# A cached-attention decode kernel on one core: each K and V tile loaded by two transfers, one from SP and one from ScalarE

## The chip, the core and the metric

The kernel runs on one core of a Trainium2 chip. The metric is the device time of one execution in microseconds (us); less is better. Engines are named as in the profile: PE (TensorE matmul), PEld (its weight load), DVE (VectorE), ACT (ScalarE), POOL (GpSimd) and SP (SyncE). SPq and ACTq are the instructions by which SP and ScalarE start DMA transfers.

## The reference

One token goes through a pre-norm attention layer with a cache and a gated feed-forward layer, all in float32. The attention, cut to what matters:

```python
B, Sq, D = 1, 1, 640
H, Sk, Dh = 32, 8192, 192
q = (layernorm(x) @ wq).reshape(B, Sq, H, Dh)           # one query row for each head
scores = einsum("bhqd,bhkd->bhqk", q, k_cache) * Dh ** -0.5
p = softmax(scores)
o = einsum("bhqk,bhkd->bhqd", p, v_cache)
h = x + o.reshape(B, Sq, H * Dh) @ wo
out = h + ((relu(hn @ W_gate) * (hn @ W_up)) @ W_down)   # hn = layernorm(h), F = 1536
```

For each of 32 heads the kernel reads 6 MB of K and 6 MB of V, and uses each element once.

## The kernel before

**Tiles.** The 8192 keys of a head are spread over 128 partitions, 64 keys of 192 numbers in each, so a K tile or a V tile is 128 x 12288 float32: 6144 KB, 48 KB in each partition. `TW` is half of a row's numbers (6144). All tiles come from one pool, `kv`, of three buffers (`kv_t`), which also holds the three pieces of wq at the start and the feed-forward weights (`ffn_a`, `ffn_b`) at the end. The output weights wo are loaded in nine pieces (`wo_t`, for groups of four heads, the last two groups of two heads) into a pool of two buffers.

**Loading.** `load_kv` (L77) takes a buffer and issues one transfer for each entry of `parts`, all from SP. Every K tile and all V tiles but the last are one transfer of 6144 KB; the last V tile is five. `load_wo` (L86) issues one transfer of 1920 KB (960 KB for the last two groups). SP does nothing but issue transfers, in order; it waits before each until the buffer is free.

**One head.** For head h+1 `head_step` (L176) multiplies the K tile by the query in four quarters of 16 keys per partition (L183, DVE), adds the two halves of each product on POOL (L184), and sums what is left on DVE (L188). Between the quarters it runs the steps of the softmax of head h (`softmax_steps`: maximum L193, its transpose on PE L195, L198, its broadcast L200, then on ScalarE the bias L202 and the exponential L205, the sum on PE L207 and its reciprocal L210). Then `values_of` (L217 on) does 32 matmuls of 128x2 by 128x384 with the V tile (L225) and ScalarE scales the result (L228). `finish_steps` brings the head's row into columns (L240, L244) and, once for each group, multiplies by wo (L254).

**What sets the order.** Instructions of one engine run in the order in which a scheduler put them; the calls `keep(...)` hold the marked DVE and PE instructions in the order of the program. The scheduler also decides which of the three buffers a tile gets, and so for what a transfer waits. In the kernel before, a V tile follows a K tile in its buffer (its transfer waits for DVE's sums, L188), and a K tile follows a V tile (its transfer waits for PE's L225).

**End.** The feed-forward weights come into two of the buffers (L294 to L298), the row is normalised and multiplied, and the result goes out (L348).

Of the kernel before, what the change touches and what calls it, by code (L numbers as in the profile page):

```python
# [14 lines left out]
def kernel(  # L15
# [12 lines left out]
    nc = tc.nc  # L28
# [9 lines left out]
    TW = R * DH  # L38
# [11 lines left out]
    kf, vf = kc[0], vc[0]  # L50
# [20 lines left out]
    for j in range(0, DJ, 2):  # L71
        n = min(2, DJ - j)
# [4 lines left out]
    def load_kv(src, h, parts):  # L77
        t = kv.tile([P, 2 * TW], F32, name="kv_t")
        v = src[h].rearrange("(p r) d -> p (r d)", p=P)
        b = 0  # L80
        for n in parts:
            nc.sync.dma_start(t[:, b:b + n], v[:, b:b + n])  # L82
            b += n
        return t

    def load_wo(gi):  # L86
        hs = GROUPS[gi]
        j = len(hs) * DH // P
        t = wts.tile([P, j, D], F32, tag="wo_t", name="wo_t")
        r0 = hs[0] * DH  # L90
        nc.sync.dma_start(t, wo[r0:r0 + len(hs) * DH, :].rearrange("(p j) n -> p j n", p=P))
        return t
# [73 lines left out]
    def query(h):  # L166
        g, i = divmod(h, HPQ)
        q = ps_q.tile([P, QB], F32, tag="q", name="q")
        nc.tensor.matmul(q[:, 0:DH], sel[:, g, :], q4[:, i * DH:(i + 1) * DH], start=True, stop=True)  # L169
        return q[:, 0:DH]  # L170
# [5 lines left out]
    def head_step(q, kt, *works):  # L176


        sc = small.tile([P, NS], F32, name="sc")
        k3 = kt.rearrange("p (r d) -> p r d", d=DH)  # L180
        parts = [(i0, k3[:, i0:i0 + SUB, :]) for i0 in range(0, NS, SUB)]
        for i0, ks in parts:
            keep(nc.vector.tensor_mul(ks, ks, q[:, None, :].to_broadcast([P, SUB, DH])))  # L183
            nc.gpsimd.tensor_add(ks[:, :, 0:HD], ks[:, :, 0:HD], ks[:, :, HD:DH])  # L184
            for w in works:
                next(w, None)
        for i0, ks in parts:
            keep(nc.vector.reduce_sum(sc[:, i0:i0 + SUB], ks[:, :, 0:HD], axis=AX.X))  # L188
        return sc

    def softmax_steps(sc, res):
        mp = small.tile([P, 1], F32, name="mp")
        keep(nc.vector.reduce_max(mp, sc, axis=AX.X))  # L193
        pt = ps_s.tile([P, 512], F32, name="ps_small")
        keep(nc.tensor.transpose(pt[0:1, 0:P], mp, ident))  # L195
        yield
        m1 = small.tile([1, 1], F32, name="m1")
        keep(nc.vector.reduce_max(m1, pt[0:1, 0:P], axis=AX.X))  # L198
        pb = ps_s.tile([P, 512], F32, name="ps_small")
        nc.tensor.matmul(pb[:, 0:1], ones[0:1, :], m1, start=True, stop=True)  # L200
        nb = small.tile([P, 1], F32, name="nb")
        nc.scalar.mul(nb, pb[:, 0:1], -SCALE)  # L202
        p = small.tile([P, NS], F32, name="p")
        rs = small.tile([P, 1], F32, name="rs")
        nc.scalar.activation(p, sc, AF.Exp, bias=nb, scale=SCALE, accum_out=rs)  # L205
        pl = ps_s.tile([P, 512], F32, name="ps_small")
        nc.tensor.matmul(pl[:, 0:1], ones, rs, start=True, stop=True)  # L207
        yield
        rl = small.tile([P, 1], F32, name="rl")
        keep(nc.vector.reciprocal(rl, pl[:, 0:1]))  # L210
        res += [p, rl]
        yield
# [8 lines left out]
    def values_of(h, p, rl, vt):  # L221
        po = pos[h % 2]
        for i in range(NP):
            g = i % NQ
            nc.tensor.matmul(po[g * Q:g * Q + 2, :], p[:, 2 * i:2 * i + 2],  # L225
                             vt[:, 2 * i * DH:(2 * i + 2) * DH], start=(i < NQ), stop=(i >= NP - NQ))
        ob = small.tile([P, 2 * DH], F32, name="ob")
        nc.scalar.activation(ob, po, AF.Copy, scale=rl)  # L228
        return ob

    def finish_steps(h, ob, oT, wo_t):

        gi, i = group_of[h]
        U = NQ // len(GROUPS[gi])
        W = DH // U
        pt = ps_s.tile([P, 512], F32, name="ps_small")
        for u in range(U):
            q0 = (i * U + u) * Q
            for k in range(2):
                nc.tensor.matmul(pt[q0:q0 + Q, 0:W], par[:, k, :], ob[:, k * DH + u * W:k * DH + (u + 1) * W],  # L240
                                 start=(k == 0), stop=(k == 1))
        yield
        s = slice(i * U * Q, (i + 1) * U * Q)
        keep(nc.vector.transpose(oT[s], pt[s, 0:W].rearrange("p (c j) -> p j c", c=Q)))  # L244
        yield
        split = h >= H - 2
        if not split and i < len(GROUPS[gi]) - 1:
            return
        if not split:
            s = slice(0, P)  # L250
        J = wo_t.shape[1]
        for j in range(J):
            for g in range(NQ):
                nc.tensor.matmul(acc[g * Q:(g + 1) * Q, :], oT[s, j, :], wo_t[s, j, g * DG:(g + 1) * DG],  # L254
                                 start=False, stop=(h == H - 1 and j == J - 1))
        yield

    sc = head_step(query(0), load_kv(kf, 0, [2 * TW]))
    done = iter(())
    for h in range(H):  # L260
        gi, i = group_of[h]
        if i == 0:
            wo_t = load_wo(gi)
            oT = small.tile([P, len(GROUPS[gi]) * DH // P, Q], F32, tag="oT", name="oT")
        sm = []
        soft = softmax_steps(sc, sm)
        if h + 1 < H:
            kt = load_kv(kf, h + 1, [2 * TW])
            vt = load_kv(vf, h, [2 * TW])
            sc = head_step(query(h + 1), kt, soft, done)  # L270
        else:
            vt = load_kv(vf, h, [TW] + [TW // 4] * 4)
        for w in (soft, done):
            for _ in w:
                pass
        done = finish_steps(h, values_of(h, *sm, vt), oT, wo_t)
# [99 lines left out]
```

## Time and profile before

| | |
|---|---|
| median of 3 runs | 1045.99 us (1045.82 to 1046.0) |
| the profiled execution's own time | 1045.67 us |
| its span in the profile | 1043.9 us |
| busy: DVE / POOL / PE / ACT | 666.0 / 440.1 / 409.2 / 45.5 us |
| bytes moved by DMA | 446.39 MB, mean 428 GB/s |
| mean granted clock of TensorE | 0.641 |

The span is what the profiler saw between the first and the last instruction; 1.8 us of the profiled execution lie outside of it. A busy share is an average over the whole span. A timeline row gives start, length, engine, line, operation, tile, and in brackets how long the engine had been idle before it and what ended that. In a table of stretches the last three columns are the granted clock, the busy share of the 16 DMA engines, and GB/s; bytes are booked to the moments in which rows start, so short stretches jump about the mean, with shares above 1 too.

### The profile page before, as it was taken

To read this page: it belongs to the slowest core of one execution; us is meant where nothing else is said; L and a number is where in the kernel's file an instruction comes from. 1 tells how busy PE (TensorE), PEld (TensorE's weight loads), DVE (VectorE), ACT (ScalarE), POOL (GpSimd) and SP (SyncE) were. 2 spreads that over 40 slices of the span, in tenths; PEclk is the share of its full clock that TensorE was granted. 3 is DMA by queue.
4 is the path that set the end of the run, shared out by engine and by line. 5 is a ranking of instruction groups with operands and counts; after the bars stand their busy time and mean duration, and the time that the engine had idled before them with its cause. 6 is when DMAs were issued, how large, how long until landed. Compare 5 with 4: busy or idle time off the path is not lost.

```text
span 1043.9 us, 7403 instructions
## 1 busy us (share of the span) xinstructions
PE 409.2 (39%) x3136; PEld 151.0 (14%) x3136; DVE 666.0 (64%) x418; ACT 45.5 (4%) x140; POOL 440.1 (42%) x139
## 2 busy tenths in 40 slices
PE   1603443343345333343432443343233444432475
PEld 0101111111112111121111111121111211111122
DVE  1086777566667766467775666677664667766551
ACT  0000000000000000000000000000000000000010
POOL 0055555344455544245553444455542455544330
PEclk9856665666666566666666666665566666656678
DMA  9999999999999999999999999999999999999997
GB/s 392 445 433 428 424 444 426 435 426 443 426 432 428 439 430 422 438 432 433 428 437 430 435 428 436 429 434 428 433 424 443 430 433 434 428 432 428 435 419 302
DMA packets 13003, 446.39 MB, mean 428 GB/s; under 512 B 1573, under 2 KB 1577, under 8 KB 3114
## 3 DMA queue, kind: packets, MB, share of 16 engines
q1 hardware_dynamic: 12824, 445.92, 99.2%
q8 instruction: 24, 0.39, 0.2%
q14 instruction: 9, 0.07, 0.0%
q10 hardware_dynamic: 146, 0.01, 0.0%
HBM read 445.91 MB, written 0.00 MB: 427 GB/s over the span
## 4 chain that ended last, share of the span: by engine, by line
DMA 62%; DVE 24%; PE 10%; issue 3%; SPq 0%; ACTq 0%; ACT 0%; DVEq 0%
DMA kv_t<-in_A_k_cache_dram 57%; DVE kv_t L183 19%; PE po L225 8%; DVE sc L188 3%; DMA xrow<-in_A_x_dram 2%; DMA ffn_b<-in_B_W_down_dram 2%; DMA ffn_a<-in_B_W_up_dram 2%; PE q L169 1%; PE qp L160 1%; DVE oT L244 1%; DVE m L198 0%; DVE rl L210 0%; DVE mp L193 0%; SPq L82 0%; PE acc L150 0%
## 5 line engine op out<-in xcount | busy, mean ns | idle before, releaser
L184 POOL TENSOR_TENSOR kv_t<-kv_t 128x1536 f32<-128x1536 f32 x128 | 438.2, 3445 | 559.6 <-DVE mp L193 247.4
L183 DVE TENSOR_TENSOR kv_t<-kv_t,q 128x3072 f32<-128x3072 f32 x128 | 427.4, 3342 | 321.1 <-DMA kv_t<-in_A_k_cache_dram 311.5
L225 PE MATMUL po<-kv_t,p 128*2 128x384 f32 x2048 | 224.4, 601 | 9.7 <-DMA kv_t<-in_A_v_cache_dram 9.7
L188 DVE TENSOR_REDUCE sc<-kv_t 128x16 f32<-128x1536 f32 x128 | 215.0, 1739 | 0.0
L195 PE MATMUL ps_small<-ident,mp 128*1 128x128 f32 x32 | 11.8, 368 | 367.6 <-DVE mp L193 367.6
L169 PE MATMUL q<-q,sel 128*128 128x192 f32 x64 | 29.6, 565 | 148.9 <-DVE kv_t L183 148.9
L225 PEld LDWEIGHTS po<-kv_t,p 128*2 128x2 f32 x2048 | 54.7, 97 | 168.9 <-issue 154.3
L195 PEld LDWEIGHTS ps_small<-ident,mp 128*1 128x1 f32 x32 | 2.5, 79 | 389.6 <-issue 355.5
L240 PE MATMUL ps_small<-ob,par 128*32 128x192 f32 (+1 forms) x144 | 44.5, 479 | 0.7 <-ACT ob L228 0.7
L200 PE MATMUL ps_small<-m,ones 1*128 1x1 f32 x64 | 18.4, 354 | 51.9 <-DVE m L198 51.9
L169 PEld LDWEIGHTS q<-q,sel 128*128 128x128 f32 x64 | 14.9, 289 | 156.1 <-DVE kv_t L183 107.5
L228 ACT ACTIVATE ob<-po,rl 128x384 f32<-128x384 f32 x32 | 18.6, 580 | 432.3 <-PE po L225 432.3
L254 PE MATMUL acc<-wo_t,oT 128*32 128x160 f32 (+1 forms) x408 | 33.5, 452 | 0.4 <-DVE oT L244 0.4
L202 ACT ACTIVATE nb<-ps_small 128x1 f32<-128x1 f32 x32 | 5.5, 171 | 495.6 <-PE ps_small L200 495.6
L200 PEld LDWEIGHTS ps_small<-m,ones 1*128 1x128 f32 x64 | 15.7, 303 | 71.8 <-DVE m L198 71.8
L207 PE MATMUL ps_small<-rs,ones 128*128 128x1 f32 x64 | 18.6, 359 | 18.9 <-ACT p L205 18.9
L254 PEld LDWEIGHTS acc<-wo_t,oT 128*32 128x32 f32 (+1 forms) x408 | 18.7, 157 | 6.9 <-DVE oT L244 1.3
L160 PE MATMUL qp<-kv_t,xn 128*32 128x512 f32 x120 | 17.4, 736 | 5.3 <-DMA kv_t<-in_A_wq_dram 4.3
L207 PEld LDWEIGHTS ps_small<-rs,ones 128*128 128x128 f32 x64 | 15.8, 308 | 24.9 <-ACT p L205 24.9
L240 PEld LDWEIGHTS ps_small<-ob,par 128*32 128x32 f32 x144 | 16.7, 153 | 16.9 <-issue 7.5
L244 DVE STREAM_TRANSPOSE oT<-ps_small 32x192 f32<-32x192 f32 (+1 forms) x32 | 11.7, 364 | 10.4 <-PE ps_small L240 9.8
L205 ACT ACTIVATE p<-sc,nb 128x64 f32<-128x64 f32 x32 | 11.1, 348 | 1.0
(72 smaller groups left out, 73.4 us busy)
## 6 DMA issues: line engine op xcount, KB each, us to landing
kv_t<-in_A_k_cache_dram SPq DMA_DIRECT2D x32, 6144.0 KB, 37.0
kv_t<-in_A_v_cache_dram SPq DMA_DIRECT2D x31, 6144.0 KB, 23.1
wo_t<-in_A_wo_dram SPq DMA_DIRECT2D x7, 1920.0 KB, 27.0
kv_t<-in_A_wq_dram SPq DMA_DIRECT2D x2, 6144.0 KB, 17.8
ffn_a<-in_B_W_up_dram SPq DMA_DIRECT2D x1, 3840.0 KB
kv_t<-in_A_wq_dram SPq DMA_DIRECT2D x1, 3072.0 KB, 39.6
kv_t<-in_A_v_cache_dram SPq DMA_DIRECT2D x1, 3072.0 KB, 31.0
kv_t<-in_A_v_cache_dram SPq DMA_DIRECT2D x4, 768.0 KB, 34.6
```

Source lines behind the costliest of these rows:

```text
L160: nc.tensor.matmul(qps[b][g * Q:(g + 1) * Q, :], xn[:, j:j + 1].to_broadcast([P, Q]), wq_ts[j][:, c0:c0 + QB], start=(j == 0), stop=(j == ...
L169: nc.tensor.matmul(q[:, 0:DH], sel[:, g, :], q4[:, i * DH:(i + 1) * DH], start=True, stop=True)
L183: keep(nc.vector.tensor_mul(ks, ks, q[:, None, :].to_broadcast([P, SUB, DH])))
L184: nc.gpsimd.tensor_add(ks[:, :, 0:HD], ks[:, :, 0:HD], ks[:, :, HD:DH])
L188: keep(nc.vector.reduce_sum(sc[:, i0:i0 + SUB], ks[:, :, 0:HD], axis=AX.X))
L200: nc.tensor.matmul(pb[:, 0:1], ones[0:1, :], m1, start=True, stop=True)
L207: nc.tensor.matmul(pl[:, 0:1], ones, rs, start=True, stop=True)
L225: nc.tensor.matmul(po[g * Q:g * Q + 2, :], p[:, 2 * i:2 * i + 2], vt[:, 2 * i * DH:(2 * i + 2) * DH], start=(i < NQ), stop=(i >= NP - NQ))
L228: nc.scalar.activation(ob, po, AF.Copy, scale=rl)
L240: nc.tensor.matmul(pt[q0:q0 + Q, 0:W], par[:, k, :], ob[:, k * DH + u * W:k * DH + (u + 1) * W], start=(k == 0), stop=(k == 1))
L244: keep(nc.vector.transpose(oT[s], pt[s, 0:W].rearrange("p (c j) -> p j c", c=Q)))
L254: nc.tensor.matmul(acc[g * Q:(g + 1) * Q, :], oT[s, j, :], wo_t[s, j, g * DG:(g + 1) * DG], start=False, stop=(h == H - 1 and j == J - 1))
```

## The change

`load_kv` gives each entry of `parts` an issuing engine. With two parts the first goes to SP and the second to ScalarE; with any other number all stay on SP. Every K tile and all V tiles but the last are now called with two parts of `TW` numbers, so 3072 KB each, 24 KB of each partition's row.

```diff
-        for n in parts:
-            nc.sync.dma_start(t[:, b:b + n], v[:, b:b + n])
+        for n, eng in zip(parts, (nc.sync, nc.scalar) if len(parts) == 2 else (nc.sync,) * len(parts)):
+            eng.dma_start(t[:, b:b + n], v[:, b:b + n])
             b += n
...
-    sc = head_step(query(0), load_kv(kf, 0, [2 * TW]))
+    sc = head_step(query(0), load_kv(kf, 0, [TW, TW]))
...
-            kt = load_kv(kf, h + 1, [2 * TW])
-            vt = load_kv(vf, h, [2 * TW])
+            kt = load_kv(kf, h + 1, [TW, TW])
+            vt = load_kv(vf, h, [TW, TW])
```

The scheduler also moves other things. In the rows below the names in brackets are the semaphores for which an instruction waits: DVE, PE, Pool and Activation for the work of these engines, DMAHW for transfers.

SP before, around the third piece of wo: K of head 8, V of head 7, wo, K of head 9, V of head 8.

```order
L82 DMA kv_t<-in_A_k_cache_dram 128x12288 [waits DMAHW3_49,PE_49]
L82 DMA kv_t<-in_A_v_cache_dram 128x12288 [waits DMAHW7_49,DMAHW4_49,DVE_49]
L91 DMA wo_t<-in_A_wo_dram 128x3840
L82 DMA kv_t<-in_A_k_cache_dram 128x12288 [waits DMAHW5_49,PE_49]
L82 DMA kv_t<-in_A_v_cache_dram 128x12288 [waits DMAHW6_49,DVE_49]
```

SP now, around the same piece: the first halves of K of head 5, V 4, K 6, then wo, V 5, K 7.

```order
L82 DMA kv_t<-in_A_k_cache_dram 128x6144 [waits DMAHW2_49,DMAHW1_49,DVE_49]
L82 DMA kv_t<-in_A_v_cache_dram 128x6144 [waits DMAHW7_49,DMAHW0_49,PE_49]
L82 DMA kv_t<-in_A_k_cache_dram 128x6144 [waits DMAHW6_49,DMAHW5_49,DVE_49]
L91 DMA wo_t<-in_A_wo_dram 128x3840 [waits PE_49]
L82 DMA kv_t<-in_A_v_cache_dram 128x6144 [waits DMAHW4_49,DMAHW3_49,PE_49]
L82 DMA kv_t<-in_A_k_cache_dram 128x6144 [waits DMAHW2_49,DMAHW1_49,DVE_49]
```

The tiles' buffers have changed hands: V waits for PE and K for DVE, so V tiles now share one buffer, each waiting for the matmuls of the V tile before it, and K tiles take turns in the other two. wo stands between a K and a V half, three heads earlier than it did, and waits for the group of wo two before it. Nothing on ScalarE's list matches wo: it is on SP alone.

ScalarE before, in two heads:

```order
L202 ACTIVATE nb<-ps_small 128x1 [waits PE_49]
L205 ACTIVATE p,rs<-sc,nb 128x64 [waits DVE_49,Activation_49]
L228 ACTIVATE ob<-po_217,rl 128x384 [waits DVE_49,PE_49]
L202 ACTIVATE nb<-ps_small 128x1 [waits PE_49]
L205 ACTIVATE p,rs<-sc,nb 128x64 [waits DVE_49,Activation_49]
L228 ACTIVATE ob<-po_216,rl 128x384 [waits DVE_49,PE_49]
```

ScalarE now, with the second halves of the tiles:

```order
L202 ACTIVATE nb<-ps_small 128x1 [waits PE_49]
L82 DMA kv_t<-in_A_k_cache_dram 128x6144 [waits DMAHW2_49,DVE_49]
L205 ACTIVATE p,rs<-sc,nb 128x64 [waits Activation_49]
L228 ACTIVATE ob<-po_217,rl 128x384 [waits DVE_49,PE_49]
L82 DMA kv_t<-in_A_v_cache_dram 128x6144 [waits DMAHW5_49,DMAHW1_49,DMAHW0_49]
L202 ACTIVATE nb<-ps_small 128x1 [waits PE_49]
```

The K half of head h+2 stands between the bias and the exponential of head h, and the V half of head h+1 behind the scaling of head h's result, with no wait for PE of its own, since that scaling has waited.

PE before, in one head (q is the query of a later head, po the product with V):

```order
L169 MATMUL q<-q_212,sel 128x192 [waits DVE_49]
L225 MATMUL po_216<-kv_t,p 2x384 [waits DMAHW2_49]
L225 MATMUL po_216<-kv_t,p 2x384 x31
L195 MATMUL ps_small<-ident,mp 1x128 [waits DVE_49,PE_49]
L240 MATMUL ps_small<-ob,par 32x192 [waits Activation_49]
```

PE now, in one head:

```order
L225 MATMUL po_216<-kv_t,p 2x384 [waits DMAHW4_49]
L225 MATMUL po_216<-kv_t,p 2x384 x15
L225 MATMUL po_216<-kv_t,p 2x384 [waits DMAHW5_49]
L225 MATMUL po_216<-kv_t,p 2x384 x15
L169 MATMUL q<-q_212,sel 128x192 [waits DVE_49]
L195 MATMUL ps_small<-ident,mp 1x128 [waits DVE_49]
L240 MATMUL ps_small<-ob,par 32x192 [waits Activation_49]
```

The 32 products with V wait twice, for the first half of the tile and after 16 of them for the second, and they come ahead of the query's copy.

## The prediction

> **What bounds the kernel now.** I read the page first, for who is busy and what the chain that ended last consists of.
>
> ```profile
> span 1043.9 us, 7403 instructions
> ...
> DMA  9999999999999999999999999999999999999997
> GB/s 392 445 433 428 424 444 426 435 426 443 426 432 428 439 430 422 438 432 433 428 437 430 435 428 436 429 434 428 433 424 443 430 433 434 428 432 428 435 419 302
> ...
> q1 hardware_dynamic: 12824, 445.92, 99.2%
> ...
> DMA 62%; DVE 24%; PE 10%; issue 3%; SPq 0%; ACTq 0%; ACT 0%; DVEq 0%
> ...
> L225 PE MATMUL po<-kv_t,p 128*2 128x384 f32 x2048 | 224.4, 601 | 9.7 <-DMA kv_t<-in_A_v_cache_dram 9.7
> ```
>
> No compute engine is near full, and the DMA engines are full in every slice but the last. SP's queue (q1) alone fills 99.2% of them. So the time is 445.92 MB over the rate, plus the start and the drain. The table of stretches says whether the rate has room: the whole middle, then a head without wo, then a head with it.
>
> ```profile
> 60.00:980.00 920.00, 350.13 (x2586) 129.38 (x2586) 632.70 (x366) 37.07 (x121) 423.97 (x124) 0.62 1.00 432
> 254.69:283.75 29.06, 11.51 (x75) 3.91 (x75) 20.63 (x13) 1.19 (x4) 13.68 (x4) 0.62 1.00 433
> ...
> 283.75:317.35 33.60, 10.64 (x75) 3.77 (x75) 20.64 (x13) 1.19 (x4) 13.68 (x4) 0.60 1.00 431
> ```
>
> The share is 1.00 and the rate 432 GB/s throughout. A head takes 29.06 us for two tiles (12.58 MB), so a tile passes in about 14.5 us; wo adds 4.54 us for its 1.97 MB, again 433 GB/s. wo's rows are 15 KB long and K's 48 KB, so shorter rows cost nothing here. The change can lose time only where the DMA engines run out of queued work. How much is queued ahead is read from the timeline of one head:
>
> ```profile
> 254.69 3.35 DVE L183 TENSOR_TENSOR kv_t<-kv_t,q 128x3072 f32<-128x3072 f32 x1 [8.71 <-DMA kv_t<-in_A_k_cache_dram]
> ...
> 262.99 0.58 PE L207 MATMUL ps_small<-rs,ones 128*128 128x1 f32 x2 [0.73 <-ACT p L205]
> 265.31 0.16 DVE L210 RECIPROCAL rl<-ps_small 128x1 f32<-128x1 f32 x1
> ...
> 268.64 6.72 DVE L188 TENSOR_REDUCE sc<-kv_t 128x16 f32<-128x1536 f32 x4
> ...
> 269.72 7.61 PE L225 MATMUL po<-kv_t,p 128*2 128x384 f32 x64
> ...
> 275.39 0.33 SPq L82 DMA_DIRECT2D kv_t<-in_A_v_cache_dram  x1
> ...
> 275.77 0.43 SPq L91 DMA_DIRECT2D wo_t<-in_A_wo_dram  x1
> ...
> 277.40 0.33 SPq L82 DMA_DIRECT2D kv_t<-in_A_k_cache_dram  x1
> ...
> 283.75 3.35 DVE L183 TENSOR_TENSOR kv_t<-kv_t,q 128x3072 f32<-128x3072 f32 x1 [8.38 <-DMA kv_t<-in_A_k_cache_dram]
> ```
>
> A K tile lands at 254.69 and the next at 283.75. SP issues the next V when DVE has summed the K tile (275.39), which is 8.4 us before what is moving has landed. That 8.4 us is the cover. Nothing in the middle waits for an engine; DVE has 8.38 us to spare.
>
> **Part 1: twice the transfers, two issuers.** SP's issues (0.33 us each) lie in its waiting. On ScalarE one K half is issued between the bias and the exponential. The nearest prices are its own two transfers at the start:
>
> ```profile
> 0.75 1.34 SPq L74 DMA_DIRECT2D kv_t<-in_A_wq_dram  x3
> ...
> 1.19 0.55 ACTq L66 DMA_DIRECT2D xrow<-in_A_x_dram  x1
> ```
>
> At 0.55 us the exponential, and the sum behind it on PE, come that much later. The sum ended at 263.57 and DVE takes it at 265.31, after its third quarter: 1.7 us of slack hide it. Without that slack it would come out of DVE's 8.38 us. The K half on ScalarE waits for DVE's sums of a tile two heads older, done 8.4 us before the newer tile landed, so it holds up nothing. The V half stands behind L228 and waits for nothing more. Price: 0.
>
> **Part 2: V behind V.** V tiles now share one buffer, and each V half waits for the last matmul of the tile before. In a head without wo, V lands 14.5 us after K, the matmuls take 224.4 / 32 = 7.0 us, and the next V halves are issued at 21.5 us, 7.5 us before the next K lands. The cover shrinks from 8.4 to 7.5 us and holds. PE copies the next query behind these matmuls, 1 us later, also in time. Price: 0.
>
> **Part 3: wo on one of two queues.** This decides. How two queues share the DMA engines is seen at the start, where x (20 B in each of 128 rows) goes out on ScalarE's queue beside wq (48 KB rows) on SP's:
>
> ```profile
> L65 ACTq DMA_DIRECT2D xT<-in_A_x_dram x1: 410/410/410, 0.7 to 0.7; - x1
> ...
> DMA to landing us min/median/max: 18.0/18.0/18.0
> ```
>
> ```profile
> 1.00:1.50 0.50, 0.00 (x0) 0.00 (x0) 0.40 (x3) 0.00 (x0) 0.47 (x2) 1.00 0.00 0
> 1.50:2.00 0.50, 0.00 (x0) 0.00 (x0) 0.38 (x1) 0.23 (x1) 0.45 (x3) 1.00 2.99 885
> ```
>
> The first bytes move about 0.75 us after the first issue at 0.75. x needs 18.0 us for 2.5 KB. Spread evenly, each of 16 engines has 8 rows of x, and a 48 KB row at 433/16 = 27 GB/s takes 1.8 us. Eight rows of x plus its semaphore, one after each row of wq, make 9 x 1.8 = 16.3 us, plus the start: 17 to 18. So the queues take turns by rows, whatever their length. [...] The trace agrees, with 18.0 us.
>
> By turns, a transfer of 128 rows costs its queue 8 turns, long or short. wo is an extra transfer on SP alone, so after each wo ScalarE's queue is one transfer ahead: wo runs beside the second half of V, then the first half of V beside the second half of the next K, then the first half of that K alone. That last half is all that is queued when V has landed: 3.146 MB at 433 GB/s, 7.26 us. The next V halves can move only after the landing is known, the 7.0 us of matmuls, the issue and the start. The two delays I take from the 0.75 us above and from the last transfer:
>
> ```profile
> 1041.12 0.65 SPq L348 DMA_DIRECT2D out_dram<-o  x1
> ```
>
> ```profile
> SPq L371 <- DMA out_dram<-o: 1.0, 1, 1.0
> ```
>
> From issue to known landing a tiny transfer took 0.65 + 1.0 = 1.7 us. So 7.0 + 1.7 - 7.26 = 1.4 us in which both queues are empty. SP's next K half can't fill it: it stands behind the waiting V half. ScalarE's next K half stands behind a bias that waits for that very K tile. After the gap both queues start level, until the next wo. Eight of the nine wo transfers (all but the first, which comes ahead of the steady heads) give 8 x 1.4 = 11 us.
>
> Bounds: if ScalarE's last row has its turn after SP's, a 24 KB row (0.9 us) is still to come and the gap is 0.5 us: 4 us in all. Upwards, "landed" means the slowest of 16 engines. How far they drift apart shows in the drain at the end, where no new work comes:
>
> ```profile
> 1034.00:1036.00 2.00, 1.40 (x36) 0.97 (x32) 0.00 (x0) 0.00 (x0) 0.00 (x0) 0.88 0.70 285
> 1036.00:1038.00 2.00, 1.44 (x24) 0.73 (x20) 0.00 (x0) 0.00 (x0) 0.00 (x0) 0.50 0.56 223
> 1038.00:1040.00 2.00, 1.87 (x40) 1.20 (x32) 0.00 (x0) 0.00 (x0) 0.00 (x0) 0.77 0.26 99
> ```
>
> The mean engine is idle 0.60 + 0.88 + 1.48 = 3.0 us there. If every gap cost that too, it would be 8 x 4.4 = 35 us. I take 11 us, since an engine that lags always is already in the rate of 432.
>
> **Part 4: start and end.** K of head 0 shares the DMA engines with the rest of wq and half of K of head 1, and may land up to one half (7.3 us) later; the bytes are the same and more is queued behind. At the end the last V tile and the feed-forward weights are all on SP, in the old order. Price: 0.
>
> Sum: the profiled execution's 1045.67 us (0.3 below the median of the runs) + 11 = 1057 us.
>
> **Rivals.**
> - *No gap, no change (0.20).* If the queues shared by bytes, 1.97 MB of V would have moved beside wo, and when V's first half landed 1.18 MB of the second K half would be left beside the first: 4.33 MB, 10.0 us, more than the 8.7 us needed. The gap also closes if the matmuls take under 5.6 us. Then the time is 1046. For it: the margin is only 1.4 us. Against it: the 18.0 us of x. [...]
> - *Faster (0.14).* No gap, two queues run the DMA engines at 433 where the middle has 432 (920 us x 1/433 = 2.1 us), and the engines drift less, at most the 3.0 us of the drain: 1041. Against it: wo's short rows already move at 433 GB/s, and the drain's transfers are unchanged.
> - *Every gap also costs the drift (0.14).* 35 us, 1081. For it: a tile is used only when the slowest engine has landed it. It decides if the slowest engine is another one each time.
> - *ScalarE's queue stalls the softmax:* the K half between bias and exponential would have to wait more than 1.7 us for DVE. Its tile was done 8.4 us earlier; I give it no chance of its own.
>
> **How the numbers follow.** Forecast (gaps of 0.5 to 2.5 us, 1050 to 1066): 0.52. The rivals: 0.20, 0.14 and 0.14. The range takes in the forecast, no change, and part of the two outer cases: 1043 to 1072. Faster or slower by over 0.2% (2.1 us, about what a measurement of this kernel can tell): faster 0.14, same 0.20, slower 0.52 + 0.14 = 0.66.
>
> **What would show it.** Right: in the stretch behind each wo the DMA share falls below 1.00 for 1 to 3 us, just before V halves are issued; eight such places, some 120 us apart; V's first half lands well after its second there; heads between them take 29.1 us; SP's waits move from DVE's L188 to PE's L225. Wrong: a share of 1.00 through the groups of four heads (then the gap isn't there), heads without wo longer than 29.1 us (then two queues cost rate everywhere), or an end later by a drain that has grown.

## The result, and the profile after

The changed kernel took 1077.87 us (median of 4 runs, 1073.54 to 1082.78), against 1045.93 us before: 1.0307 times as long, with a 95% interval of 1.0262 to 1.0351. The forecast was slower, 1057 us, in a range that ended at 1072; the time lies beyond it. The profiled execution took 1078.3 us.

The page of the changed kernel, the lines that answer to those of before:

```profile
span 1076.5 us, 7479 instructions
...
DMA  9999999998999989999899989999899998999997
GB/s 404 422 428 430 429 399 425 435 424 356 436 429 428 429 364 430 431 427 431 352 429 432 429 358 435 428 433 427 360 432 430 429 431 370 433 428 430 409 423 331
...
q1 hardware_dynamic: 12824, 247.73, 54.4%
q10 hardware_dynamic: 9218, 198.19, 43.0%
...
DMA 77%; PE 23%; issue 0%; SPq 0%; DVE 0%
DMA kv_t<-in_A_v_cache_dram 69%; PE po L225 22%; DMA kv_t<-in_A_wq_dram 4%; DMA ffn_b<-in_B_W_down_dram 2%; DMA ffn_a<-in_B_W_up_dram 1%; PE qp L160 1%; SPq L74 0%; PE pd L344 0%; DVE o L347 0%; PE ps_small L195 0%
...
L225 PE MATMUL po<-kv_t,p 128*2 128x384 f32 x2048 | 241.9, 640 | 260.3 <-DMA kv_t<-in_A_v_cache_dram 260.3
```

The rate has eight notches, at the slices with 399, 356, 364, 352, 358, 360, 370 and 409 GB/s. A slice is 26.9 us; against 430 GB/s they miss 31 + 74 + 66 + 78 + 72 + 70 + 60 + 21 = 472, and 472 / 430 x 26.9 = 29.5 us. That is nearly all of the 32.6 us by which the span grew. The notch at 364 GB/s, 66 / 430 x 26.9 = 4.1 us, is the one looked at below; the first is smaller, and so are the last two, which stand behind the wo of half the size. The chain of work now runs from V's transfer to V's products and on to the next V: no head passes without it. One of the notches on the timeline (SPq and ACTq are the issues):

```profile
348.01 0.33 SPq L82 DMA_DIRECT2D kv_t<-in_A_v_cache_dram  x1
...
348.10 0.34 ACTq L82 DMA_DIRECT2D kv_t<-in_A_v_cache_dram  x1
...
380.93 8.05 PE L225 MATMUL po<-kv_t,p 128*2 128x384 f32 x64 [17.40 <-DMA kv_t<-in_A_v_cache_dram]
388.20 3.35 DVE L183 TENSOR_TENSOR kv_t<-kv_t,q 128x3072 f32<-128x3072 f32 x1 [13.38 <-DMA kv_t<-in_A_k_cache_dram]
...
389.05 0.33 SPq L82 DMA_DIRECT2D kv_t<-in_A_v_cache_dram  x1
...
389.14 0.34 ACTq L82 DMA_DIRECT2D kv_t<-in_A_v_cache_dram  x1
```

and the same place in stretches of half a microsecond (PE busy with its count, granted clock, DMA share, GB/s):

```profile
380.50:381.00 0.50, 0.07 (x4) 0.50 0.92 393
...
385.50:386.00 0.50, 0.50 (x9) 0.50 0.92 393
386.00:386.50 0.50, 0.50 (x8) 0.55 0.12 49
386.50:387.00 0.50, 0.50 (x12) 1.00 0.23 98
387.00:387.50 0.50, 0.50 (x12) 1.00 0.00 0
...
389.50:390.00 0.50, 0.00 (x1) 1.00 0.00 0
390.00:390.50 0.50, 0.00 (x0) 1.00 3.49 786
```

V is issued at 348.01 and usable at 380.88. PE starts at once, but the DMA engines run dry at 386.0, with the products half done. They end at 389.0, the next V is issued at 389.05, and bytes move again from about 390.2. In these 4.2 us three rows of 24 KB start (the 49 and 98 GB/s), where at 430 GB/s it would be over 70. The chain over three heads shows that this comes with wo:

```profile
287.71 22.09 DMA kv_t<-in_A_v_cache_dram
309.80 0.04 issue
309.84 7.81 PE po L225 x64
317.66 0.02 issue
317.67 22.09 DMA kv_t<-in_A_v_cache_dram
...
339.80 8.19 PE po L225 x64
...
348.01 32.87 DMA kv_t<-in_A_v_cache_dram
```

From issue to landing a V tile takes 22.09 us, the one behind wo 32.87 us: 10.8 us more for 1.97 MB. wo's 8 rows of 15 KB for each engine, each taking turns with a 24 KB row of V, make 8 x 39 KB at 27 GB/s = 11.8 us; sharing by bytes would make 2 x 1.97 MB at 430 GB/s = 9.2 us. The trace also records the queue of every single row, and that settles it: from 352.1 to 364.3 us the 128 rows of wo pass on SP's queue beside 130 rows of 24 KB on ScalarE's, one for one. From 380 to 386 us every row of 24 KB that starts belongs to SP's half of the K tile, which travels alone.

### The profile page after: what moved, and what is told of

It reads as the page before. It is cut to its first block, busy times and chain, and to the rows that moved or that the text cites. A ratio compares the mean times of both kernels' runs of the same rounds, so it can differ in the third digit from the quotient of the medians.

```text
span 1076.5 us, 7479 instructions
## 1 busy us (share of the span) xinstructions
PE 405.7 (38%) x3136; PEld 144.8 (13%) x3136; DVE 666.7 (62%) x418; ACT 45.6 (4%) x140; POOL 440.1 (41%) x139
## 4 chain that ended last, share of the span: by engine, by line
DMA 77%; PE 23%; issue 0%; SPq 0%; DVE 0%
DMA kv_t<-in_A_v_cache_dram 69%; PE po L225 22%; DMA kv_t<-in_A_wq_dram 4%; DMA ffn_b<-in_B_W_down_dram 2%; DMA ffn_a<-in_B_W_up_dram 1%; PE qp L160 1%; SPq L74 0%; PE pd L344 0%; DVE o L347 0%; PE ps_small L195 0%
## 5 line engine op out<-in xcount | busy, mean ns | idle before, releaser
L225 PE MATMUL po<-kv_t,p 128*2 128x384 f32 x2048 | 241.9, 640 | 260.3 <-DMA kv_t<-in_A_v_cache_dram 260.3
L225 PEld LDWEIGHTS po<-kv_t,p 128*2 128x2 f32 x2048 | 57.4, 102 | 424.5 <-DMA kv_t<-in_A_v_cache_dram 263.4
L240 PE MATMUL ps_small<-ob,par 128*32 128x192 f32 (+1 forms) x144 | 41.2, 452 | 0.7 <-ACT ob L228 0.7
L169 PE MATMUL q<-q,sel 128*128 128x192 f32 x64 | 19.2, 385 | 21.7 <-DVE kv_t L183 21.7
L254 PE MATMUL acc<-wo_t,oT 128*32 128x160 f32 (+1 forms) x408 | 27.1, 435 | 0.4 <-DVE oT L244 0.4
L207 PEld LDWEIGHTS ps_small<-rs,ones 128*128 128x128 f32 x64 | 14.8, 289 | 29.7 <-ACT p L205 27.4
L169 PEld LDWEIGHTS q<-q,sel 128*128 128x128 f32 x64 | 9.9, 194 | 42.5 <-issue 41.8
```

## The experiments

The theory, as the prediction had it: behind each wo ScalarE's queue is one transfer ahead, so only half a K tile is queued when V has landed, and the next V waits for the products. Its rivals after the result: two queues cost rate everywhere; V behind V is enough by itself; short rows or more transfers cost rate. In each list of runs the kernel before was timed on the same chip, at 1045.6 to 1045.8 us.

**One queue, V behind V.** All halves on SP, the buffers held by hand as in the changed kernel.

```diff
-        for n, eng in zip(parts, (nc.sync, nc.scalar) if len(parts) == 2 else (nc.sync,) * len(parts)):
+        for n, eng in zip(parts, (nc.sync,) * len(parts)):
...
-        t = kv.tile([P, 2 * TW], F32, name="kv_t")
+        n = 0 if src is vf and h == H - 1 else 2 if src is vf else h % 2
+        t = kv.tile([P, 2 * TW], F32, tag=f"kv{n}", name="kv_t")
```

> All halves are issued by SP; the buffers are held as in the changed kernel (V behind V, K in the other two). Theory of turns (a wo transfer on one of two queues puts the other queue one transfer ahead, so that only half a K tile is queued when V has landed): with one queue nothing gets ahead, 1046 to 1048 us, DMA share 1.00 through every group. Rival, V behind V is enough by itself: gaps of some 4 us stay, 1070 to 1080. Rival, halves cost rate (rows of 24 KB): 1055 or more with no gaps.

Measured: 1050.47 us, 1.0045 times before (1.003 to 1.006). No notch is left, so the gaps need the second queue. But 4.7 us stay, more than I had expected: the middle runs at 430 GB/s, where before had 432.

```profile
60.00:980.00 920.00, 385.09 (x2586) 131.92 (x2586) 626.92 (x364) 37.05 (x121) 416.85 (x122) 0.64 1.00 430
```

**Halves with the old buffers, and whole tiles with the new.** The first is the changed kernel with the line of the loop as above and nothing else; the scheduler then gives the buffers as before. The second keeps V behind V and loads whole tiles (`[2 * TW]`) from SP.

> Halves, all issued by SP, and the scheduler gives the buffers as in the kernel before (V behind K, K behind V). The one-queue kernel with V behind V took 1050.5 us with no gaps and a rate of 429.9 GB/s in place of 432.4. If the halves cost that rate: 1050 to 1051 again. If V behind V costs it: 1046.

> Whole tiles, one transfer each from SP, with V behind V as in the changed kernel. If the halves cost the rate: 1046. If V behind V costs it: 1050 to 1051.

Measured: 1050.52 us (1.0045, 1.0028 to 1.0062) and 1045.79 us (1.0001, 0.9991 to 1.001). So V behind V costs nothing on one queue, and the halves cost 4.7 us under either order of the buffers. In the second kernel the middle is back at its rate:

```profile
60.00:980.00 920.00, 347.68 (x2586) 129.25 (x2586) 632.54 (x366) 37.09 (x121) 423.97 (x124) 0.62 1.00 432
```

**wo on both queues.** wo is cut like K and V.

```diff
-        nc.sync.dma_start(t, wo[r0:r0 + len(hs) * DH, :].rearrange("(p j) n -> p j n", p=P))
+        wv = wo[r0:r0 + len(hs) * DH, :].rearrange("(p j) n -> p (j n)", p=P)
+        tv = t.rearrange("p j n -> p (j n)")
+        c = j * D // 2
+        nc.sync.dma_start(tv[:, 0:c], wv[:, 0:c])
+        nc.scalar.dma_start(tv[:, c:2 * c], wv[:, c:2 * c])
```

> The changed kernel with wo cut as K and V are: half of it on SP, half on ScalarE. Theory of turns: both queues get the same number of turns, no queue gets ahead, no gaps: 1046 to 1051. Rival, two queues cost rate or ScalarE's waits hold transfers back: the time stays near 1078, since the same number of bytes goes over the same two queues.

Measured: 1051.58 us (1.0055, 1.004 to 1.007): 26.3 us of the loss are gone with two queues still there. The chain of this kernel shows a V tile without and with wo beside it:

```profile
253.05 22.19 DMA kv_t<-in_A_v_cache_dram
...
341.25 26.32 DMA kv_t<-in_A_v_cache_dram
```

wo now adds 4.1 us to V's way, about its bytes (4.6 us at 430 GB/s) and nothing for a queue that got ahead.

**wo on ScalarE, and V's second half first.** Two ways to have half of the products done before the late half of V lands.

```diff
-        nc.sync.dma_start(t, wo[r0:r0 + len(hs) * DH, :].rearrange("(p j) n -> p j n", p=P))
+        nc.scalar.dma_start(t, wo[r0:r0 + len(hs) * DH, :].rearrange("(p j) n -> p j n", p=P))
```

```diff
-        for i in range(NP):
+        for n in range(NP):
+            i = (n + NP // 2) % NP
             g = i % NQ
...
-                             vt[:, 2 * i * DH:(2 * i + 2) * DH], start=(i < NQ), stop=(i >= NP - NQ))
+                             vt[:, 2 * i * DH:(2 * i + 2) * DH], start=(n < NQ), stop=(n >= NP - NQ))
```

> The changed kernel with each wo issued by ScalarE in place of SP. Theory of turns: now SP's queue gets ahead by one transfer. The first half of V then lands first and PE does 16 of the 32 products while the second half is under way, so behind its landing only 16 are left (4.0 us in place of 8.0): 4.0 + 1.7 - 7.3 is below zero, with 1.5 us of drift just about zero: 1046 to 1054. Rival, any unevenness of the queues opens a gap: near 1078.

> The changed kernel with the second half of each V tile (ScalarE's, which lands first behind a wo) multiplied first. The transfers are the same. Theory of turns: ScalarE's queue is still one transfer ahead behind each wo, but behind the landing of the late half only 16 products are left, 4.0 us less: gaps of 0 to 1 us in place of 3.9, 1046 to 1054. Rival, the gap comes from the queues alone and not from the products that the next V waits for: unchanged, near 1078.

Measured: 1061.43 us (1.0145, 1.013 to 1.0161) and 1059.94 us (1.0133, 1.0116 to 1.015). Against the 1050.5 of halves without gaps the changed kernel loses 27.4 us, 3.4 for each of eight wo, and these two lose 11.0 and 9.5; both times lie beyond the 1046 to 1054 that were expected. The first has seven notches and the second six, so some 1.6 us for each: the gap shrinks with the products, as the theory says, but not to zero. Two rows of the first kernel's chain say the larger part of why:

```profile
252.86 4.89 PE po L225 x32
...
375.88 4.82 PE po L225 x32
```

Half of the products takes 4.9 us and not 4.0. The eighth notch of the first kernel is missing because ScalarE issues the second wo at 22.9 us there, ahead of the steady heads. The two places without a notch in the second kernel are those of the wo of half the size.

**No wo.** Only the first group's wo is loaded and serves all groups.

```diff
-            wo_t = load_wo(gi)
+            if gi == 0:
+                wo_all = load_wo(gi)
+            wo_t = wo_all[:, 0:len(GROUPS[gi]) * DH // P, :]
```

> The changed kernel with only the first group's wo loaded (and used for all groups): eight transfers, 13.8 MB, are left out, so part of the sum over heads is wrong. At 432 GB/s these bytes are 32 us. Theory of turns: no wo, no gap, 1046 - 32 = 1014 to 1017. Rival, two queues cost rate everywhere or V behind V makes gaps by itself: 1078 - 32 = 1046.

> The kernel before with the same eight wo transfers left out (the same part of the sum is wrong), as the measure for the two others of this kind: 1046 - 32 = 1014 by every theory.

Measured, one run each: 1022.19 us for the changed kernel without them, 1013.52 for the kernel before. The gaps at the eight places are gone. Of the 8.7 us between the two, 4.7 are the price of the halves; one notch near 104 us takes the other 4.0. It comes behind the first wo, the one that I had left out of the count; no run shows that this wo makes it. In the changed kernel the engines stay busy there, with the second wo issued at 81.3 us.

**Short transfers in wo's place.** The kernel without wo, with a transfer of 128 short rows on SP at each place: rows of 64 bytes, then of 4 KB.

```diff
+            else:
+                nc.sync.dma_start(wo_all[:, 0, 0:16], wo[gi * P:(gi + 1) * P, 0:16])
```

> As the changed kernel without the eight wo transfers, but at each of their places SP issues a transfer of 128 rows of 64 bytes into the wo tile (8 KB in place of 1920; the same part of the sum is wrong). Theory of turns: a transfer of 128 rows costs its queue as many turns as any other, so ScalarE's queue still gets one transfer ahead and the gaps of 3 to 5 us are back: 1014 + 8 x 3.9 = 1045, with under 0.1 MB more moved than without. If the queues share by bytes: no lead, 1014 to 1017.

> As the kernel with the 8 KB transfers in place of wo (1031.4 us against 1022.2 without them), but with 512 KB: 128 rows of 4 KB (the same part of the sum is wrong, in its numbers too). The bytes alone add 4.2 MB, 9.7 us: 1032. Theory of turns with a full turn for each row: a lead of a whole transfer less 0.5 MB, gaps of some 3.9 us at seven places, 1059. If short rows pass more than one to a turn, as the 64 byte rows seem to do: about 1041. If the queues share by bytes: 1032, no gaps.

Measured, one run each: 1031.4 and 1037.32 us. So 8 KB, issued eight times, cost 9.2 us, which no sharing by bytes explains. The gaps are where they should be; the same stretch without and with the 64 byte rows:

```profile
488.00:494.00 6.00, 0.27 (x1) 0.08 (x1) 3.81 (x3) 0.00 (x0) 0.32 (x1) 0.50 1.01 434
```

```profile
488.00:494.00 6.00, 2.09 (x22) 0.58 (x14) 1.58 (x1) 0.58 (x1) 0.00 (x0) 0.99 0.78 270
```

But they are smaller than the 31 us that was expected: 9.2 us. With the 4 KB rows the difference is 15.1 - 9.7 for the bytes = 5.4 us, and the notch near 104 us is nearly gone in that kernel (411 GB/s in its slice of 25.9 us, 369 without wo), so its own gaps cost more, 5.4 + 42 / 430 x 25.9 = 7.9 us. In these kernels V behind a short transfer takes (64 bytes, then 4 KB)

```profile
218.00 26.15 DMA kv_t<-in_A_v_cache_dram
```

```profile
216.37 28.14 DMA kv_t<-in_A_v_cache_dram
```

so 4.1 and 6.1 us more than 22.09, where eight full turns would add 7.3 and 8.4. It isn't that a short row costs less than a turn: by the records of the single rows ScalarE's queue moves 132 rows of 24 KB between the first and the last of the 128 rows of 64 bytes at this place, and 136 beside those of 4 KB (130 beside wo's in the changed kernel). But 128 short rows are few bytes (8 or 512 KB in place of 1920), and so ScalarE's queue is empty soon: in the kernel with 64 bytes the second half of V has landed at 233.4 us, the next K half is issued at 233.84 and moves from about 237, and until then SP's rows move alone and make up for a part of the lead. In the changed kernel ScalarE's next K half is issued at 362.06, before wo and the half of V beside it are through (364 to 366).

**Buffers dealt out in turn.** Meant to put V behind K again with two queues.

```diff
-    kv = ctx.enter_context(tc.tile_pool(name="kv", bufs=3))
+    kv = ctx.enter_context(tc.tile_pool(name="kv", bufs=1))
+    turn = iter(range(1000))
+
+    def kv_tile(name):
+        return kv.tile([P, 2 * TW], F32, tag=f"kv{next(turn) % 3}", name=name)
```

> The changed kernel with the three buffers dealt out in turn, as the kernel before had them: V behind K and K behind V, still two queues, wo still on SP. Theory of turns: ScalarE's queue gets ahead in the same way, but when V lands the next K is queued whole and the next V waits only for DVE's sums of the K tile that is landed (20.7 us behind it), against three halves of transfers (21.8 us): 20.7 + 1.7 + 1.5 of drift - 21.8 leaves 0.6 to 2.1 us a group, 1050 to 1063. If V behind V were no part of the cause: near 1078.

Measured: 1333.69 us (1.2763, 1.2742 to 1.2785). This doesn't answer what it was made for: the scheduler put the K transfer that waits for V's products ahead of the V transfer that doesn't, so in every head nothing is queued while PE works. It gives the loop's price in the clear:

```profile
299.23 7.89 PE po L230 x64
...
307.13 0.33 SPq L87
...
307.51 32.02 DMA kv_t<-in_A_v_cache_dram
339.53 0.04 issue
339.57 8.19 PE po L230 x64
```

K is issued first, at 307.13. From there to V's landing at 339.53 pass 32.4 us for two tiles, which at 430 GB/s take 29.3 us. So 3.1 us go to the start and to the wait until the landing is known, and the products at these two places take 7.9 and 8.2 us.

**Two halves by partitions.** One queue, V behind V, each tile cut between partitions 63 and 64.

```diff
+        if len(parts) == 2:
+            for p0 in (0, P // 2):
+                nc.sync.dma_start(t[p0:p0 + P // 2, :], v[p0:p0 + P // 2, :])
+            return t
```

> As the one-queue kernel with V behind V, but each tile is cut between partitions 63 and 64 in place of in the middle of its rows: as many transfers (two a tile), rows of 48 KB. If the lost rate hangs on the number of rows: 1046. If it hangs on the number of transfers: 1050 to 1051. If half the partitions at a time are slower by themselves: more than that.

Measured: 2060.06 us (1.9688, 1.9659 to 1.9717). It says nothing on rows against transfers, since half the partitions at a time moved at about half the rate, 211 GB/s against 432:

```profile
60.00:1980.00 1920.00, 364.81 (x2595) 133.10 (x2595) 642.26 (x370) 37.10 (x121) 425.73 (x125) 0.56 1.00 211
```

So no run separates more rows from more transfers. The durations of the single rows in the traces point to the rows: a 48 KB row takes 1818 ns (median, kernel before), a 24 KB row 914 (one queue, V behind V), so two halves take 2 x 914 - 1818 = 10 ns more than a whole. Each engine moves 63 x 8 = 504 more rows, which makes 5.0 us. The entry of 4 bytes that ends each transfer takes 9 ns on each engine, 0.6 us for 63 more transfers.

## Why the prediction was wrong

*What bounds the kernel:* right. The DMA engines are the bound (their share was 1.00 in the middle of the kernel before, at 432 GB/s), and only what leaves them without work or slows them counts.

*Part 1, twice the transfers for nothing:* wrong by 4.7 us. The failing sentence is the one in "What bounds the kernel now", that shorter rows cost nothing. It rested on the 4.54 us of wo, the difference of two periods (33.60 and 29.06); an error of 0.02 us in it is as large as the 0.5% in question. Two kernels with halves on one queue show 430 in place of 432 GB/s, and single rows 10 ns of their own. ScalarE's part of it was right: the K half is issued in 0.33 us between bias and exponential, ScalarE idles 0.29 us there (at 146.7 us), and the chain of work above has no step on ACT.

*Part 2, V behind V for nothing:* right on one queue (1045.79 us). With two queues no run takes it alone: the kernel with the buffers dealt out in turn changed more than that.

*Part 3, the gap behind each wo:* the mechanism was right: eight notches some 126 us apart, gone when wo goes over both queues, smaller when half of the products are done early. The size failed: 1.4 us was forecast, and 29.5 / 8 = 3.7 measured, 4.1 at the one shown. The failing step is the sum 7.0 + 1.7 - 7.26: both of its first terms were too small, and the sentence that a lagging engine "is already in the rate of 432" put the drift of the engines at nothing.

At the gap shown above the products took 8.1 us and not 7.0: the granted clock stands at 0.50 for the first five microseconds and at 1.00 only then. PE had idled for 17.4 us, but that isn't shown to be the reason: the products of the head before took 8.19 us after an idle time of 3.75. The 7.0 was a mean over heads, which is 241.9 / 32 = 7.6 in the changed kernel.

The delays came to 3.4 us and not to 1.7: the half K tile, 7.3 us long, was used up 5.1 us after V was known to have landed, so 2.2 of it had gone by then, and from the issue until the engines moved bytes again it took 1.2 (sixteen rows start at 390.02 to 390.30). With these 8.1 + 3.4 - 7.3 = 4.2, as the stretches show. Most of the 2.2 is the drift. The trace stamps when each of the 16 engines reports its part of a transfer: of this V half the first did at 377.37, the mean one at 378.99 and the last at 380.88, so the tile could be used 1.9 us after the mean engine had gone on. Behind the third to the ninth wo it is 1.7 to 3.7 us. I had taken the landing's delay from a transfer of 2.5 KB. V in the kernel before has such a drift too, 1.3 to 3.1 us from the mean engine to the last, and loses nothing by it, since its DMA engines never run out of queued work (a share of 1.00 from 60 to 980 us). So the rival at 1081 us, with 3.0 us of drift in each gap, came near in its reason as well as in its time; the products at the low clock, 1.1 us here, it did not have.

*Part 4, start and end for nothing:* the last slice moves 331 GB/s where it moved 302, so the drain is about 29 / 430 x 26.9 = 1.8 us shorter. The sum: 29.5 for the gaps + 4.7 for the halves - 1.8 = 32.4, against 32.6 measured.

*The rivals:* "no gap, no change" fell with the eight notches. Two queues brought no bandwidth (430 GB/s from 266 to 386 us, between two gaps, where the kernel before had 432), but the order in which the halves land changed with them (V's second half near 366 us, its first at 380.88), and the gaps that came of it were worth 27 us (1077.87 against 1050.47 on one queue). "Faster" fell: the engines ran at 430 and not at 433 GB/s.

*The range* was too narrow on the long side: 8 x the upper price of a gap was 35 us, and I kept it at a chance of 0.14 although the middle value took a mean for the products and a tiny transfer for the delay.

## What to carry to other kernels

Two queues that each carried half of every tile stayed level here only while they carried the same number of rows, short or long, since they took turns by rows (130 rows of 24 KB beside the 128 of wo, 132 beside 128 rows of 64 bytes); a third transfer on one of them put the other ahead, and the last half of a tile then travelled alone (from 380 to 386 us 104 rows started on SP's queue and none on ScalarE's). So before a split, count what else goes over each queue, and what is queued when the late half lands: the work between landing and the next issue, at the clock that PE gets then (0.50 for five microseconds here), plus what the start and the slowest DMA engine take (3.4 us here), must be less than that. In this kernel, which is at its DMA rate (a share of 1.00 at 432 GB/s), one whole transfer for each tile on one queue lost nothing (1045.79 us with V behind V, 1.0001 times before), and no variant tried here that does the whole work was faster than the kernel before.

## What the runs showed of the hardware that was not expected

A tile cut by partitions (64 rows of 48 KB, twice) moved at 211 GB/s with a DMA share of 1.00, half of the 432 of the whole tile. Two such transfers, issued one behind the other on one queue, didn't make up for each other: the 211 GB/s are the mean over 1920 us of them. No run shows why.

A tile cut along its rows, with all 128 partitions in both halves, lost 0.5% of the rate (432 to 430 GB/s): by the single rows' durations, some 10 ns for each row on its engine, at each of four lengths (medians: 1818 ns for 48 KB, 914 for 24 KB, 575 for 15 KB, 293 for 7.5 KB).

The 16 DMA engines don't land their parts of a tile together: in the kernel before the last did so 1.3 to 3.1 us after the mean one for V. With work queued behind, the DMA share stayed at 1.00 there; in the changed kernel it was paid where the engines ran out of work before a transfer that waited for the tile (1.9 us in the gap of 4.2 shown above).
